# Operand loads in fewer pieces and moved against the steps, and a GpSimd cast in place of the values' casting loads

## The chip, the cores and the metric

The kernel runs on one core of a Trainium2 chip. The metric is the device time of one execution in microseconds. Before the change three executions took 695.05, 695.21 and 695.46 us, a median of 695.21. A further execution was profiled: it took 694.12 us, of which the trace spans 692.2 us from the first to the last instruction.

## The reference

```python
def _attn_ref(q, k, v, centroids):            # q, k, v: (2, 8, 768, 64), float32
    q_n = q / (norm(q) + 1e-6); k_n = ...; c_n = ...
    q_assign = argmax(einsum('bhsd,hcd->bhsc', q_n, c_n)); k_assign = ...   # 16 clusters a head
    mask = q_assign[:, :, :, None] == k_assign[:, :, None, :]
    scores = where(mask, scale * q @ k^T, -1e9)
    scores -= max(scores)
    attn = exp(scores); attn /= sum(attn) + 1e-9
    return attn @ v
def _moe_ref(x, U, V, w_ch1, w_ch2):          # mixing over tokens, then a feed-forward layer
    u = x + (x^T @ U @ V)^T
    return u + relu(u @ w_ch1) @ w_ch2
def _moe2_ref(x, w_in, conv_w, w_out):        # a gated layer with a convolution of width 3
    h = relu(x @ w_in)
    return (h * sigmoid(conv3(h))) @ w_out
```

The whole is `_moe2_ref(_moe_ref(attention))`. The change touches the attention alone.

## The kernel before, in words

The program has three stages: attention (from the start to about 300 us), the feed-forward layer, and the gated layer. In the attention two heads form a pair (index b for the batch, p for the pair, j = 0 or 1 for the head within it); there are 8 pairs, and each head has 6 query tiles of 128 rows. One query tile is one step n, so there are 96 steps, 12 to a pair; s is a step's number within its pair.

A product of float32 precision is made of two parts of the type fp32r, a rounded high half and the low half, which is the difference between the number and its rounded half. For scores the kernel keeps two tiles for each head. `cd` holds the rounded q and k on partitions 0 to 63 (and cluster rows on 64 to 79, which do the masking). `ab` holds 128 partitions: low q beside rounded k on one half of the partitions, rounded q beside low k on the other. One product with `ab` (L342) and one with `cd` (L353) give the scores of a step.

The rounded parts come by DMAs issued on the GpSimd queue, which cast while they move. `load_ops` (L108) loads the same 384 KB of one head three times: into both halves of `ab` and into `cd`. `load_raw` (L89) brings the unrounded rows of a pair (tiles rq, rk) by SyncE's queue. `split_ops` (L124) turns half of `ab` into low parts: two GpSimd subtractions for each head, raw minus rounded, in place. The values go the same way: `load_v` (L115) loads them unrounded into rv on SyncE's queue and rounded into vt with two casting DMAs on GpSimd's queue, and a GpSimd subtraction (L532, L633) puts the low half beside the rounded one.

A step (function `step`, L644) issues, in this order: the scores of step n + 2; a third of the value product of a group of three steps (`pv_mm`); on every third step the transposes that end a group (`fin_t`); the transposes of the exponentials (`t_mm`, L380); on ScalarE and VectorE their rounding and low half (`t_hi` L389, `t_lo` L393); the exponential of step n + 1 and the maximum of n + 2. At steps with (n - 4) divisible by 3, GpSimd adds 1e-9 to a group's three sums (L681), and `fin_x` (L423) ends the group before it: ScalarE copies the transposed result from PSUM into the tile `ats` (L426), VectorE takes the reciprocal of the sums (L429), GpSimd adds the two halves (L430) and multiplies by the reciprocal into X (L434, three times). The tile `ats` has one buffer, so ScalarE's next copy waits for GpSimd's last multiplication.

`prep` (L610) prepares the next pair beside the current one: loads of head 0 at s = 0, its split at s = 2, the values' loads at s = 3, loads of head 1 at s = 4 and its split at s = 5, cluster rows at s = 6, and the values' low half at s = 8. Before the loop, lines 526 to 532 do the same for the second head of pair 0 and its values. Every engine runs its instructions in the order in which they are written here; there is no scheduler. `a_ab` has 3 buffers, so at most three heads' operands live at once; rq, rk and vt have 2, rv has 1.

Of the kernel before, what the change touches and what calls it, by code (L numbers as in the profile page):

```python
# [15 lines left out]
F32 = mybir.dt.float32  # L16
# [8 lines left out]
P = 128  # L25
# [6 lines left out]
def tile_kernel(ctx: ExitStack, tc: tile.TileContext, qk, vv, cen, u_w, v_w, w1, w2, win, wout, conv, out):  # L32
    nc = tc.nc
    B, H, D, _, S = qk.shape
    NC = cen.shape[0] // H
    NP = H // 2
# [31 lines left out]
    a_e = att.enter_context(tc.tile_pool(name="a_e", bufs=3))  # L68
# [16 lines left out]
    raw = {}  # L85
    ops = {}
    vts = {}

    def load_raw(b, p, parts=1):  # L89
        rq, rk = raw[b, p] if (b, p) in raw else take_raw(b, p)  # L90
        h0 = 2 * p
        for i in range(parts):
            c = slice(i * S // parts, (i + 1) * S // parts)
            nc.sync.dma_start(out=rq[:, c], in_=qk[b, h0:h0 + 2, :, 0, c].rearrange("h d s -> (h d) s"))
            nc.sync.dma_start(out=rk[D:2 * D, c], in_=qk[b, h0, :, 1, c])
            nc.sync.dma_start(out=rk[0:D, c], in_=qk[b, h0 + 1, :, 1, c])

    def take_raw(b, p):
        raw[b, p] = tuple(a_raw.tile([P, S], F32, tag=t, name=t) for t in ("rq", "rk"))
        return raw[b, p]  # L100

    def take_ops(b, p, j):
        ab = a_ab.tile([P, 2, S], F32R, tag="ab", name="ab")
        cd = a_ab.tile([80, 2, S], F32R, tag="cd", name="cd")
        ops[b, 2 * p + j] = (ab, cd)
        return ab, cd

    def load_ops(b, p, j):  # L108
        h = 2 * p + j
        ab, cd = take_ops(b, p, j)  # L110
        nc.gpsimd.dma_start(out=ab[0:D], in_=qk[b, h])
        nc.gpsimd.dma_start(out=ab[D:2 * D], in_=qk[b, h])
        nc.gpsimd.dma_start(out=cd[0:D], in_=qk[b, h])

    def load_v(b, p):  # L115
        rv = a_v.tile([P, 2, NT, D], F32, tag="rv", name="rv", bufs=1)
        vt = a_v.tile([P, 2, NT, 2 * D], F32R, tag="vt", name="vt")
        nc.sync.dma_start(out=rv, in_=vv[b, p])
        for j in range(2):
            nc.gpsimd.dma_start(out=vt[:, j, :, 0:D], in_=vv[b, p, :, j])  # L120
        vts[b, p] = vt
        return rv, vt

    def split_ops(b, p, j, eng):  # L124
        rq, rk = raw[b, p]
        ab, _ = ops[b, 2 * p + j]
        q0, k0 = (0, D) if j == 0 else (D, 0)
        for r, i, p0 in ((rq, 0, q0), (rk, 1, k0)):
            eng.tensor_sub(ab[p0:p0 + D, i], r[p0:p0 + D], ab[p0:p0 + D, i])


    cent = acon.tile([P, 1, D], F32, name="cent")
# [60 lines left out]
    def split_first(half, which):  # L193
        c = slice(half * HS, (half + 1) * HS)
        if which == "k":
            nc.scalar.copy(cd0[0:D, 1, c], rk0[D:2 * D, c])
            nc.scalar.copy(ab0[0:D, 1, c], rk0[D:2 * D, c])
            nc.gpsimd.tensor_copy(ab0[D:2 * D, 1, c], rk0[D:2 * D, c])
            nc.vector.tensor_sub(ab0[D:2 * D, 1, c], rk0[D:2 * D, c], ab0[D:2 * D, 1, c])
        else:  # L200
            nc.scalar.copy(cd0[0:D, 0, c], rq0[0:D, c])
            nc.scalar.copy(ab0[D:2 * D, 0, c], rq0[0:D, c])
            nc.gpsimd.tensor_sub(ab0[0:D, 0, c], rq0[0:D, c], cd0[0:D, 0, c])
# [7 lines left out]
    def sims(b, p, tiles=range(NT)):  # L211
        rq, rk = raw[b, p]
        if (b, p) not in ohst:
            ohst[b, p] = {"pm": ps_t.tile([P, NT * 4, NC], F32, tag="t", name="sim")}
        pm = ohst[b, p]["pm"]
        for t in tiles:
            for i, (r, cb) in enumerate(((rq, cbq), (rk, cbk))):
                nc.tensor.matmul(
                    pm[:, 4 * t + 2 * i:4 * t + 2 * i + 2, :].rearrange("p g c -> p (g c)"),
                    r[:, t * P:(t + 1) * P], cb[:, p], start=True, stop=True,  # L220
                )

    def sims_onehot(b, p, part):

        v = ohst[b, p]
        if part == 0:
            v["mx"] = a_oh.tile([P, NT * 4, 1], F32, tag="mx", name="mx")
            v["eq"] = a_oh.tile([P, NT * 4, NC], BF16, tag="eq", name="eq")
            v["m2"] = a_oh.tile([P, NT * 4, 1], BF16, tag="m2", name="m2")
            v["oh"] = a_oh.tile([P, NT * 4, NC], BF16, tag="oh", name="oh")  # L230
        onehot_part(v, v["pm"], slice(0, NT * 4), part)
# [15 lines left out]
    def onehot_t(b, p):  # L247
        oh = ohst[b, p]["oh"]
        pt = ps_t.tile([4 * NC, S], BF16, tag="t", name="oht")
        for t in range(NT):  # L250
            nc.tensor.transpose(pt[:, t * P:(t + 1) * P], oh[:, 4 * t:4 * t + 4].rearrange("p g c -> p (g c)"), identb)
        ohst[b, p]["pt"] = pt

    def onehot_rows(b, p):
        pt = ohst.pop((b, p))["pt"]
        os_ = a_oh.tile([4 * NC, S], F32R, tag="os", name="os")
        nc.scalar.activation(os_, pt, AF.Identity, scale=ohs[:, 0:1], bias=ohs[:, 1:2])
        put_rows(b, p, os_, range(2))

    def put_rows(b, p, os_, heads):  # L260
        for j in heads:
            cd = ops[b, 2 * p + j][1]
            for i in range(2):
                r0 = (2 * i + j) * NC
                nc.sync.dma_start(out=cd[D:D + NC, i].bitcast(F32), in_=os_[r0:r0 + NC].bitcast(F32))
# [62 lines left out]
    st = {}  # L328
    X = {}

    def head_of(n):
        b, r = divmod(n, H * NT)
        h, t = divmod(r, NT)
        return b, h, t
# [87 lines left out]

    def fin_x(g):  # L423
        b, h, t0 = head_of(3 * g)
        at = a_e.tile([P, 3, 2, D], F32, tag="ats", name="ats", bufs=1)
        nc.scalar.copy(at, st.pop(("at", g)))  # L426
        sm = st.pop(("sum", g))
        rs = a_s.tile([P, 3, 1], F32, tag="rs", name="rs")
        nc.vector.reciprocal(rs[:, :, 0], sm)  # L429
        nc.gpsimd.tensor_add(at[:, :, 0], at[:, :, 0], at[:, :, 1])  # L430
        if h == 0 and t0 == 0:
            X[b] = xp.tile([P, NT, DM], F32, tag="x", name="x")
        for i in range(3):
            nc.gpsimd.tensor_tensor(  # L434
                out=X[b][:, t0 + i, h * D:(h + 1) * D], in0=at[:, i, 0],
                in1=rs[:, i].to_broadcast([P, D]), op=ALU.mult,
            )
# [48 lines left out]
    def pump(plan):  # L486

        for j in list(fly):
            j["at"] += 1
            if j["at"] in j["plan"]:  # L490
                j["plan"][j["at"]](j)
            if j["at"] == max(j["plan"]):
                fly.remove(j)
        if plan is THIN:
            free = not fly
        else:
            free = not fly or (fly[-1]["at"] > 1 and fly[-1]["plan"] is FLOW)
        if jobs and free:
            j = jobs.pop(0)
            j["at"], j["plan"] = 0, plan  # L500
            job_dma(j)
            fly.append(j)
# [21 lines left out]


    load_ops(0, 0, 1)
    rv0 = load_v(0, 0)
    first_pair()
    split_first(1, "q")
    sims(0, 1, range(2))  # L530
    split_ops(0, 0, 1, nc.gpsimd)
    nc.gpsimd.tensor_sub(rv0[1][:, :, :, D:2 * D], rv0[0], rv0[1][:, :, :, 0:D])  # L532


    u3 = mixc.tile([P, NT, 3, R], F32, name="u3")
# [74 lines left out]
    def prep(n):  # L610

        pair, s = divmod(n, 2 * NT)
        nxt = pair + 1
        if nxt < B * NP:
            b, p = divmod(nxt, NP)
            for part, at in enumerate((2, 2, 3, 4, 5) if nxt > 1 else (0, 0, 1, 2, 3)):
                if s == at and (nxt > 1 or part > 1):
                    sims_onehot(b, p, part)
            if s == 0:
                if nxt > 1:  # L620
                    load_raw(b, p)
                load_ops(b, p, 0)
            elif s == 2:
                split_ops(b, p, 0, nc.gpsimd)
            elif s == 3:
                st["rv"] = load_v(b, p)
            elif s == 4:
                load_ops(b, p, 1)
            elif s == 5:
                split_ops(b, p, 1, nc.gpsimd)  # L630
            elif s == 8:
                rv, vt = st.pop("rv")
                nc.gpsimd.tensor_sub(vt[:, :, :, D:2 * D], rv, vt[:, :, :, 0:D])  # L633
            if s == (6 if nxt > 1 else 5):
                onehot_t(b, p)
                onehot_rows(b, p)
        if n == NQ - 7:
            queue_chunk(1, lambda: wpc)
        if n >= NQ - 7:
            pump(FLOW)  # L640
        elif n % 2 == 0 and n > 0:
            pump(THIN)

    def step(n):  # L644
# [43 lines left out]
        if 0 <= n < NQ:  # L688
            prep(n)
# [190 lines left out]
    for i in range(len(order) + 2):  # L880
# [7 lines left out]
        if 0 <= i - 2:  # L888
            b, f = order[i - 2]
# [57 lines left out]
```

## Time and profile before

| | us |
|---|---|
| median of three executions | 695.21 (695.05 to 695.46) |
| profiled execution, device time | 694.12 |
| its span | 692.2 |
| TensorE busy | 666.3 (96%) |
| VectorE busy | 445.8 (64%) |
| ScalarE busy | 373.0 (54%) |
| GpSimd busy | 298.9 (43%) |

Times in rows are counted from the first instruction. In a timeline row the columns are start, duration, engine, line, operation, out<-in, shapes and count, and in brackets how long the engine sat idle before it and what ended that. PE is TensorE, PEld its weight loads, DVE VectorE, ACT ScalarE, POOL GpSimd and SP SyncE. A timeline row with a count above one runs from its first instruction to its last, other engines' rows being listed between them.

### The profile page before, as it was taken

How to read it: one execution, taken by the hardware profiler on the slowest of the kernel's cores; microseconds unless marked ns; L12 is line 12 of the kernel's file. 1: busy time of each engine (PE TensorE's matmuls, PEld its weight loads, DVE VectorE, ACT ScalarE, POOL GpSimd, SP SyncE). 2: the span in 40 equal slices, each digit the busy share in tenths (PEclk: the TensorE clock that was granted, in tenths of full speed). 3: DMA queues.
4: the chain of work that ended last, by engine and by line, in shares of the span. 5: the costliest groups of instructions: out<-in, count | busy, mean ns of one | idle time of the engine just before them, and what ended most of it. 6: DMA issues, size and time to landing. Idle time of an engine off the chain costs nothing.

```text
span 692.2 us, 10474 instructions
## 1 busy us (share of the span) xinstructions
PE 666.3 (96%) x3782; PEld 586.0 (85%) x3782; DVE 445.8 (64%) x833; ACT 373.0 (54%) x750; POOL 298.9 (43%) x392
## 2 busy tenths in 40 slices
PE   8949999999999999999999999999999999999997
PEld 6849999999898998888888888888887788888886
DVE  6837888797978798749831778775237645643400
ACT  6837888787777898424311333433133457653611
POOL 6647666676666642515621333332015634332300
PEclk9988999999999999999999999999999999999999
DMA  9895768685666610301210333442003000000111
GB/s 195 151 136 115 165 116 197 108 192 103 167 119 153 131 35 5 118 31 63 92 62 1 121 123 121 142 133 92 1 30 125 28 0 1 1 32 16 43 49 46
DMA packets 32131, 61.58 MB, mean 89 GB/s; under 512 B 15856, under 2 KB 19568, under 8 KB 32080
## 3 DMA queue, kind: packets, MB, share of 16 engines
q1 hardware_dynamic: 15936, 40.08, 19.6%
q0 software_dynamic: 16144, 20.84, 17.6%
q8 instruction: 30, 0.49, 0.3%
q14 instruction: 21, 0.17, 0.1%
HBM read 56.29 MB, written 3.15 MB: 86 GB/s over the span
## 4 chain that ended last, share of the span: by engine, by line
PE 78%; DVE 8%; issue 3%; DMA 3%; ACT 3%; POOL 2%; ACTq 0%; POOLq 0%; DVEq 0%
PE g L836 10%; PE tr L380 7%; PE pv L404 7%; PE h L713 5%; PE h L715 5%; PE h L714 5%; PE a L730 5%; PE a L729 5%; PE a L731 5%; PE sc L342 3%; PE sc L353 3%; PE po L870 3%; PE po L871 3%; PE po L872 3%; DMA ab<-in_qk_dram 3%
## 5 line engine op out<-in xcount | busy, mean ns | idle before, releaser
L518 POOL TENSOR_TENSOR wl<-wx,wh 128x512 fp32r<-128x512 f32 x48 | 63.0, 1314 | 114.8 <-ACT wh L517 114.5
L393 DVE TENSOR_TENSOR pl<-tr,ph 128x384 fp32r<-128x384 f32 x192 | 97.6, 549 | 21.5 <-ACT ph L389 20.3
L380 PE MATMUL tr<-identf,e 128*128 128x128 f32 x576 | 83.7, 278 | 16.5 <-ACT ats L426 11.4
L389 ACT CAST ph<-tr 128x384 fp32r<-128x384 f32 x192 | 83.5, 485 | 21.3 <-PE tr L380 20.5
L359 DVE TENSOR_SCALAR_CACHE_REDUCE e<-sc 128x768 f32<-128x768 f32 x96 | 90.8, 947 | 0.6 <-PE sc L353 0.6
L718 ACT ACTIVATE rh<-h 128x512 fp32r<-128x512 f32 (+1 forms) x52 | 29.3, 563 | 111.7 <-PE h L715 111.7
L371 ACT ACTIVATE e<-sc,nb 128x768 f32<-128x768 f32 x96 | 88.4, 921 | 1.0 <-DVE e L359 0.9
L380 PEld LDWEIGHTS tr<-identf,e 128*128 128x128 f32 x576 | 66.9, 142 | 25.9 <-ACT ats L426 12.6
L719 DVE SCALAR_TENSOR_TENSOR rl<-h,rh 128x512 fp32r<-128x512 f32 (+1 forms) x52 | 33.7, 648 | 82.9 <-ACT rh L718 82.8
L713 PE MATMUL h<-uh,wh 128*128 128x512 f32 (+1 forms) x208 | 78.1, 376 | 1.6 <-DVE rl L719 1.6
L729 PE MATMUL a<-rh,wh 128*128 128x512 f32 (+1 forms) x208 | 78.1, 376 | 0.5 <-DVE xa L745 0.5
L730 PE MATMUL a<-rl,wh 128*128 128x512 f32 (+1 forms) x208 | 77.8, 374 | 0.5 <-DVE rl L719 0.3
L731 PE MATMUL a<-rh,wl 128*128 128x512 f32 (+1 forms) x208 | 77.6, 373 | 0.0
L715 PE MATMUL h<-uh,wl 128*128 128x512 f32 (+1 forms) x208 | 77.6, 373 | 0.0
L714 PE MATMUL h<-ul,wh 128*128 128x512 f32 (+1 forms) x208 | 77.6, 373 | 0.0
L404 PE MATMUL pv<-ph,vt 128*128 128x384 f32 x192 | 66.0, 344 | 0.2 <-ACT asb L413 0.2
L404 PE MATMUL pv<-pl,vt 128*128 128x384 f32 x192 | 65.3, 340 | 0.0
L517 ACT CAST wh<-wx 128x512 fp32r<-128x512 f32 x48 | 29.8, 620 | 58.3 <-DVE wx L471 58.1
L342 PE MATMUL sc<-ab 128*128 128x384 f32 x192 | 57.4, 381 | 0.7 <-ACT e L371 0.4
L853 POOL TENSOR_TENSOR h<-h,cv 128x768 f32<-128x768 f32 x16 | 29.6, 1850 | 64.5 <-ACT cv L852 64.5
L467 DVE SCALAR_TENSOR_TENSOR wx<-wb,wx 128x512 int32<-128x512 int32 (+3 forms) x52 | 48.3, 928 | 11.4 <-ACT wb L458 9.4
L353 PE MATMUL sc<-cd 80*128 80x384 f32 x192 | 49.7, 341 | 0.0
(136 smaller groups left out, 1493.4 us busy)
## 6 DMA issues: line engine op xcount, KB each, us to landing
raw<-in_w_dram SPq DMA_DIRECT2D x32, 512.0 KB, 3.7
ab<-in_qk_dram POOLq DMA_DIRECT2D x30, 384.0 KB, 5.2
cd<-in_qk_dram POOLq DMA_DIRECT2D x15, 384.0 KB, 6.8
raw<-in_win_dram SPq DMA_DIRECT2D x8, 512.0 KB, 3.7
raw<-in_wout_dram SPq DMA_DIRECT2D x8, 512.0 KB, 3.7
rv<-in_vv_dram SPq DMA_DIRECT2D x8, 384.0 KB, 3.4
vt<-in_vv_dram POOLq DMA_DIRECT2D x16, 192.0 KB, 3.6
out_dram<-o SPq DMA_DIRECT2D x24, 128.0 KB, 1.8
```

The source lines that it names most:

```text
L359: nc.vector.tensor_scalar(out=e, in0=ps[:, :, 0:HS], scalar1=-SCALE, scalar2=3e38, op0=ALU.mult, op1=ALU.min, accum_out=nb,)
L371: nc.scalar.activation(e, ps[:, :, 0:HS], AF.Exp, scale=SCALE, bias=nb, accum_out=st["sum", n // 3][:, n % 3:n % 3 + 1])
L380: nc.tensor.transpose(pt[:, k, :], e[:, i, k * P:(k + 1) * P], identf)
L389: nc.scalar.copy(st["pt", n // 3][0][:, i * NK:(i + 1) * NK, n % 3, :], st["t", n, i])
L393: nc.vector.tensor_sub(lo, st.pop(("t", n, i)), hi)
L404: nc.tensor.matmul(acc, vt[:, h % 2, k, :], m[:, k].rearrange("p a b -> p (a b)"), start=(k == 0 and i == 0), stop=(k == NT - 1 and i == 1),)
L713: nc.tensor.matmul(ph, wh[:, k, ws], uh[g][:, k, ts], start=(k == 0), stop=False)
L714: nc.tensor.matmul(ph, wh[:, k, ws], ul[g][:, k, ts], start=False, stop=False)
L715: nc.tensor.matmul(ph, wl[:, k, ws], uh[g][:, k, ts], start=False, stop=(k == ND - 1))
L729: nc.tensor.matmul(accs[d][:, 0:n], wh[:, i, ds_], rh, start=(f == 0), stop=False)
L730: nc.tensor.matmul(accs[d][:, 0:n], wh[:, i, ds_], rl, start=False, stop=False)
L731: nc.tensor.matmul(accs[d][:, 0:n], wl[:, i, ds_], rh, start=False, stop=(f == NH - 1))
```

## The change

`load_ops` loads two and a half pieces for each head in place of three: the whole into `cd`, the whole into the upper half of `ab`, and into the lower half of `ab` only that one of q and k which stays rounded there. The low part on the lower half is now the raw rows minus `cd`, written into `ab`; the other subtraction is as before. `load_v` keeps only SyncE's load. A new function `split_v` makes the rounded half by a GpSimd copy with a cast (L122 of the changed kernel) and then the low half (L123). The first head of pair 1 is loaded before the loop; a later pair's first head, and its raw rows, are loaded at s = 10 of the pair two before it. The split of head 0 moves from s = 2 to s = 1, the loads of head 1 from s = 4 to 3, their split from s = 5 to 7, the values' load from 3 to 4. The tile `ats` gets a second buffer.

```diff
--- before.py
+++ after.py
@@ -108,25 +108,27 @@
     def load_ops(b, p, j):
         h = 2 * p + j
         ab, cd = take_ops(b, p, j)
-        nc.gpsimd.dma_start(out=ab[0:D], in_=qk[b, h])
+        nc.gpsimd.dma_start(out=cd[0:D], in_=qk[b, h])
         nc.gpsimd.dma_start(out=ab[D:2 * D], in_=qk[b, h])
-        nc.gpsimd.dma_start(out=cd[0:D], in_=qk[b, h])
+        nc.gpsimd.dma_start(out=ab[0:D, 1 - j], in_=qk[b, h, :, 1 - j])
 
     def load_v(b, p):
         rv = a_v.tile([P, 2, NT, D], F32, tag="rv", name="rv", bufs=1)
+        nc.sync.dma_start(out=rv, in_=vv[b, p])
+        return rv
+
+    def split_v(b, p, rv):
         vt = a_v.tile([P, 2, NT, 2 * D], F32R, tag="vt", name="vt")
-        nc.sync.dma_start(out=rv, in_=vv[b, p])
-        for j in range(2):
-            nc.gpsimd.dma_start(out=vt[:, j, :, 0:D], in_=vv[b, p, :, j])
+        nc.gpsimd.tensor_copy(vt[:, :, :, 0:D], rv)
+        nc.gpsimd.tensor_sub(vt[:, :, :, D:2 * D], rv, vt[:, :, :, 0:D])
         vts[b, p] = vt
-        return rv, vt
 
     def split_ops(b, p, j, eng):
-        rq, rk = raw[b, p]
-        ab, _ = ops[b, 2 * p + j]
-        q0, k0 = (0, D) if j == 0 else (D, 0)
-        for r, i, p0 in ((rq, 0, q0), (rk, 1, k0)):
-            eng.tensor_sub(ab[p0:p0 + D, i], r[p0:p0 + D], ab[p0:p0 + D, i])
+
+        ab, cd = ops[b, 2 * p + j]
+        lo, hi = raw[b, p][j], raw[b, p][1 - j]
+        eng.tensor_sub(ab[0:D, j], lo[0:D], cd[0:D, j])
+        eng.tensor_sub(ab[D:2 * D, 1 - j], hi[D:2 * D], ab[D:2 * D, 1 - j])
 
 
     cent = acon.tile([P, 1, D], F32, name="cent")
@@ -422,7 +424,7 @@
 
     def fin_x(g):
         b, h, t0 = head_of(3 * g)
-        at = a_e.tile([P, 3, 2, D], F32, tag="ats", name="ats", bufs=1)
+        at = a_e.tile([P, 3, 2, D], F32, tag="ats", name="ats", bufs=2)
         nc.scalar.copy(at, st.pop(("at", g)))
         sm = st.pop(("sum", g))
         rs = a_s.tile([P, 3, 1], F32, tag="rs", name="rs")
@@ -527,9 +529,10 @@
     rv0 = load_v(0, 0)
     first_pair()
     split_first(1, "q")
+    load_ops(0, 1, 0)
     sims(0, 1, range(2))
     split_ops(0, 0, 1, nc.gpsimd)
-    nc.gpsimd.tensor_sub(rv0[1][:, :, :, D:2 * D], rv0[0], rv0[1][:, :, :, 0:D])
+    split_v(0, 0, rv0)
 
 
     u3 = mixc.tile([P, NT, 3, R], F32, name="u3")
@@ -616,24 +619,22 @@
             for part, at in enumerate((2, 2, 3, 4, 5) if nxt > 1 else (0, 0, 1, 2, 3)):
                 if s == at and (nxt > 1 or part > 1):
                     sims_onehot(b, p, part)
-            if s == 0:
-                if nxt > 1:
-                    load_raw(b, p)
-                load_ops(b, p, 0)
-            elif s == 2:
+            if s == 1:
                 split_ops(b, p, 0, nc.gpsimd)
             elif s == 3:
+                load_ops(b, p, 1)
+            elif s == 4:
                 st["rv"] = load_v(b, p)
-            elif s == 4:
-                load_ops(b, p, 1)
-            elif s == 5:
+            elif s == 7:
                 split_ops(b, p, 1, nc.gpsimd)
             elif s == 8:
-                rv, vt = st.pop("rv")
-                nc.gpsimd.tensor_sub(vt[:, :, :, D:2 * D], rv, vt[:, :, :, 0:D])
+                split_v(b, p, st.pop("rv"))
             if s == (6 if nxt > 1 else 5):
                 onehot_t(b, p)
                 onehot_rows(b, p)
+        if s == 10 and pair + 2 < B * NP:
+            load_raw(*divmod(pair + 2, NP))
+            load_ops(*divmod(pair + 2, NP), 0)
         if n == NQ - 7:
             queue_chunk(1, lambda: wpc)
         if n >= NQ - 7:
```

GpSimd's queue at the start of the loop, before the change, from the last piece of head 0's split (L203): ab_209 is the second head of pair 0, ab_338 and ab_450 are the two heads of pair 1, vt_215 and vt_417 the values of pairs 0 and 1.

```order
L203 TENSOR_TENSOR ab_196<-rq_111,cd_197 64x384
L129 TENSOR_TENSOR ab_209<-rq_111,ab_209 64x768
L129 TENSOR_TENSOR ab_209<-rk_112,ab_209 64x768
L532 TENSOR_TENSOR vt_215<-rv_214,vt_215 128x12x64
L111 DMA ab_338<-in_qk_dram 64x1536
L112 DMA ab_338<-in_qk_dram 64x1536
L113 DMA cd_339<-in_qk_dram 64x1536
L129 TENSOR_TENSOR ab_338<-rq_180,ab_338 64x768
L129 TENSOR_TENSOR ab_338<-rk_181,ab_338 64x768
L120 DMA vt_417<-in_vv_dram 128x6x64 x2
L681 TENSOR_SCALAR sum_302<-sum_302 128x3
```

The same place on GpSimd in the changed kernel: ab_209 and vt_291 are pair 0's, ab_279 with cd_280 and ab_415 with cd_416 the two heads of pair 1.

```order
L205 TENSOR_TENSOR ab_196<-rq_111,cd_197 64x384
L111 DMA cd_280<-in_qk_dram 64x1536
L112 DMA ab_279<-in_qk_dram 64x1536
L113 DMA ab_279<-in_qk_dram 64x768
L130 TENSOR_TENSOR ab_209<-rk_112,cd_210 64x768
L131 TENSOR_TENSOR ab_209<-rq_111,ab_209 64x768
L122 CAST vt_291<-rv_214 128x12x64
L123 TENSOR_TENSOR vt_291<-rv_214,vt_291 128x12x64
L130 TENSOR_TENSOR ab_279<-rq_180,cd_280 64x768
L131 TENSOR_TENSOR ab_279<-rk_181,ab_279 64x768
L111 DMA cd_416<-in_qk_dram 64x1536
L112 DMA ab_415<-in_qk_dram 64x1536
```

The three load issues of pair 1's first head have moved ahead of pair 0's splits, a cast stands ahead of the values' low half, and the splits of pair 1's first head follow four instructions behind its loads, not directly.

A few rows further on GpSimd, before the change: the loads of pair 1's second head (ab_450, cd_451), its split, and the first group's end (sum, ats, x).

```order
L111 DMA ab_450<-in_qk_dram 64x1536
L112 DMA ab_450<-in_qk_dram 64x1536
L113 DMA cd_451<-in_qk_dram 64x1536
L129 TENSOR_TENSOR ab_450<-rq_180,ab_450 64x768
L129 TENSOR_TENSOR ab_450<-rk_181,ab_450 64x768
L681 TENSOR_SCALAR sum_384<-sum_384 128x3
L430 TENSOR_TENSOR ats_558<-ats_558 128x3x64
L434 TENSOR_TENSOR x_563<-ats_558,rs_560 128x64 x3
L633 TENSOR_TENSOR vt_417<-rv_416,vt_417 128x12x64
```

The same place in the changed kernel, from the last of those loads (ab_415, the second head of pair 1):

```order
L113 DMA ab_415<-in_qk_dram 64x768
L682 TENSOR_SCALAR sum_306<-sum_306 128x3
L682 TENSOR_SCALAR sum_385<-sum_385 128x3
L432 TENSOR_TENSOR ats_552<-ats_552 128x3x64
L436 TENSOR_TENSOR x_557<-ats_552,rs_554 128x64 x3
L130 TENSOR_TENSOR ab_415<-rk_181,cd_416 64x768
L131 TENSOR_TENSOR ab_415<-rq_180,ab_415 64x768
L122 CAST vt_589<-rv_449 128x12x64
L123 TENSOR_TENSOR vt_589<-rv_449,vt_589 128x12x64
L682 TENSOR_SCALAR sum_472<-sum_472 128x3
```

The first group's sums and its end (ats, x) now stand between the loads and the split that waits for them; before, they stood behind that split.

## Rows read from the trace of the kernel before

**Rows 1.** The page's chain that ended last, its shares of the span by engine:
```profile
PE 78%; DVE 8%; issue 3%; DMA 3%; ACT 3%; POOL 2%; ACTq 0%; POOLq 0%; DVEq 0%
```

**Rows 2.** Busy time by stretch: bounds, length, each engine (count), clock, DMA share, GB/s:
```profile
41.00:52.00 11.00, 1.61 (x8) 0.96 (x6) 1.31 (x3) 1.36 (x4) 6.59 (x8) 0.71 0.48 82
52.00:60.00 8.00, 7.93 (x42) 7.54 (x42) 6.27 (x16) 6.29 (x15) 4.75 (x13) 0.75 0.78 187
60.00:100.00 40.00, 39.46 (x289) 38.38 (x288) 33.03 (x77) 31.32 (x74) 28.88 (x45) 1.00 0.61 119
```

**Rows 3.** Timeline of all engines, 28 to 58 us, the first group's copy and the longest gap:
```profile
33.28 0.49 ACT L426 COPY ats<-at 128x384 f32<-128x384 f32 x1
...
49.10 0.18 DVE L429 RECIPROCAL rs<-sum 128x3 f32<-128x3 f32 x1 [8.90 <-POOL sum L681]
50.64 0.48 ACT L426 COPY ats<-at 128x384 f32<-128x384 f32 x1 [11.10 <-POOL x L434]
```

**Rows 4.** Timeline of GpSimd, 14 to 56 us:
```profile
14.73 0.99 POOL L203 TENSOR_TENSOR ab<-rq,cd 64x384 fp32r<-64x384 f32 x1 [3.87 <-ACT cd L201]
...
19.98 2.00 POOL L532 TENSOR_TENSOR vt<-rv,vt 128x768 fp32r<-128x768 f32 x1 [0.21 <-POOL ab L129]
21.93 0.57 POOL L111 DMA_DIRECT2D ab<-in_qk_dram  x1
...
28.57 1.83 POOL L129 TENSOR_TENSOR ab<-rq,ab 64x768 fp32r<-64x768 f32 x1 [5.01 <-DVE e L359]
...
34.34 0.57 POOL L111 DMA_DIRECT2D ab<-in_qk_dram  x1
...
45.09 1.80 POOL L129 TENSOR_TENSOR ab<-rq,ab 64x768 fp32r<-64x768 f32 x1 [9.11 <-DMA ab<-in_qk_dram]
```

**Rows 5.** Timeline of TensorE, 39 to 59 us, step transposes of n = 10 to 13:
```profile
39.55 0.82 PE L380 MATMUL tr<-identf,e 128*128 128x128 f32 x6
51.18 1.88 PE L380 MATMUL tr<-identf,e 128*128 128x128 f32 x6 [9.39 <-ACT ats L426]
55.56 1.02 PE L380 MATMUL tr<-identf,e 128*128 128x128 f32 x6
58.14 0.82 PE L380 MATMUL tr<-identf,e 128*128 128x128 f32 x6
```

**Rows 6.** The same, 82 to 91 us, steps 22 and 25:
```profile
83.20 0.82 PE L380 MATMUL tr<-identf,e 128*128 128x128 f32 x6
...
89.72 0.82 PE L380 MATMUL tr<-identf,e 128*128 128x128 f32 x6
```

**Rows 7.** GpSimd's groups: shapes xcount | busy, mean ns | idle before, releaser:
```profile
L120 POOL DMA_DIRECT2D vt<-in_vv_dram x16 | 14.0, 880 | 1.5 <-PE pv L404 1.5
L633 POOL TENSOR_TENSOR vt<-rv,vt 128x768 fp32r<-128x768 f32 x7 | 12.9, 1842 | 0.0
L198 POOL CAST ab<-rk 64x384 fp32r<-64x384 f32 x2 | 1.0, 504 | 0.1
L541 POOL COPY u<-wx 128x192 f32<-128x192 f32 x3 | 0.9, 343 | 0.1
```

**Rows 8.** Timeline of TensorE's weight loads, first value product of pair 0:
```profile
24.00 0.19 PEld L404 LDWEIGHTS pv<-ph,vt 128*128 128x128 f32 x1
```

**Rows 9.** The tile ab: its DMAs from issue to landing:
```profile
DMA to landing us min/median/max: 3.9/5.2/10.0
```

**Rows 10.** Timeline of GpSimd, 84 to 87 us, around s = 10 of pair 1:
```profile
84.93 0.80 POOL L434 TENSOR_TENSOR x<-ats,rs 128x64 f32<-128x64 f32 x3
85.67 0.58 POOL L111 DMA_DIRECT2D ab<-in_qk_dram  x1
```

**Rows 11.** Timeline of VectorE, one instruction with two SBUF inputs, GpSimd idle, then busy:
```profile
512.89 0.69 DVE L467 SCALAR_TENSOR_TENSOR wx<-wb,wx 128x512 int32<-128x512 int32 x1
518.48 1.77 DVE L467 SCALAR_TENSOR_TENSOR wx<-wb,wx 128x512 int32<-128x512 int32 x1 [1.19 <-ACT wb L458]
```

**Rows 12.** Timeline of GpSimd, what it ran beside the second of these:
```profile
515.71 5.69 POOL L751 TENSOR_TENSOR ul<-xa,uh 128x512 fp32r<-128x512 f32 x4 [36.31 <-ACT uh L750]
```

## The prediction

> **What bounds the kernel now.** The page's chain comes first: 78% of the span is TensorE's own work, and the next largest share is 8% [rows 1]. No step of this change shortens a product, so only waits of TensorE can be won. The table of stretches, read next, shows where they lie. From 60 to 100 us TensorE is busy 39.46 of 40 us; from 41 to 52 us it is busy 1.61 of 11, and there and in the 8 us behind it the granted clock averages 0.71 and 0.75, where it is 1.00 afterwards [rows 2]. One hole, then, at the end of pair 0, with a slow stretch behind it.
>
> The timelines of this stretch say whose hole it is. TensorE's transposes of step 11 wait 9.39 us for ScalarE's copy into `ats` [rows 5]; that copy waits 11.10 us for GpSimd's multiplication of the group before, which reads the one `ats` buffer, and VectorE's reciprocal waits 8.90 us for GpSimd's sum [rows 3]. GpSimd itself had stood 9.11 us before the split of head 3 (the second head of pair 1), whose loads it had begun to issue at 34.34 us; 5.01 us more had gone before the split of head 2, for loads begun at 21.93 [rows 4]. The split stands right behind its loads on an in-order engine, and the sums and group ends stand behind the split. So what decides is GpSimd's lag in the first pair, and two other engines hang on it by two separate ties.
>
> What the hole costs: from step 10 to step 13 the transposes advance 58.14 - 39.55 = 18.59 us [rows 5]; the same four places one pair later take 89.72 - 83.20 = 6.52 us [rows 6]. The difference, **12.07 us**, holds the 9.39 us of waiting, and nearly all the rest is step 11, which takes 55.56 - 51.18 = 4.38 us at the lower of the two clock levels (1.2 of 2.4 GHz).
>
> **The change part by part.**
>
> *Head 2's loads, ahead of pair 0's splits.* GpSimd ends L203 at 14.73 + 0.99 = 15.72 us [rows 4]. It then issues two whole pieces at 0.57 us and a half piece, which lies between nothing and 0.57 [rows 4] and which I take at half: 17.2 us. The two splits of head 1 took it from there to the values' subtraction in 19.98 - 15.72 = 4.26 us, 0.3 of it waiting for a load [rows 4], so they end near 21.1. The cast of the values (128x768) does not occur before. The nearest rows are a cast of 384 elements, 0.504 us, and copies of 192, 0.343 [rows 7]; carried on by their difference this gives 0.83, by twice the cast 1.0, and I take 0.95; as an upper end it costs as much as the subtraction of the same shape, 1.84 us [rows 7], as a lower end 0.504. Then the subtraction, 2.00 us [rows 4]: the values are ready at about 24.2 to 24.4 us, with the upper end 25.3, where TensorE loads its first value weights at 24.00 [rows 8] and the values were ready at 21.98. **This cover is gone: +0.3 us**, between 0 and 1.3.
>
> *Splits of head 2.* Its loads, begun at 15.72, have 8.5 us before GpSimd comes to them at 24.4; the tile's loads take 5.2 us in the median, 10.0 at most [rows 9]. The earlier wait of 5.01 us goes. The splits end near 28.1.
>
> *Head 3's loads and its split, now parted.* The loads are issued from 28.1 to 29.7, six microseconds before their old place. Then come the sums, and the first group's end, for which ScalarE's copy is there at 33.28 + 0.49 = 33.8 [rows 3]; an addition and 0.80 us of multiplications [rows 10] keep GpSimd until about 35.2, and only then it turns to the split, two times 1.83 us [rows 4]. By the median the first piece is there at 33.3, by the maximum at 38.1, so the split waits 0 to 3 us. It ends between 38.9 and 42, the values between 41.8 and 45, the next sum a quarter of a microsecond later. VectorE asks for that sum at step 13, which without the hole is near 39.55 + 6.52 = 46 us. So even the slowest load in this trace leaves 0.8 us, and **the hole goes: -12.07 us**. Since TensorE then has no rest there, the cause of the low clock is gone too. Once it goes, the next late thing would be what binds TensorE in every pair; the reference stretch of 6.52 us already contains that.
>
> *The second buffer of `ats`.* By itself it would cut ScalarE's tie to the multiplication, but not VectorE's to the sum: the reciprocal starts at 49.10 and the copy at 50.64 [rows 3], so it is worth about 1.5 us alone. Together with the new order it adds nothing to the sum; it is slack.
>
> *The steady pairs.* The loads at s = 10 change little there: GpSimd had nothing between the multiplication of s = 10 and the loads of s = 0, and issued the loads at 85.67, directly behind the multiplication begun at 84.93 [rows 10]. Sixteen issues of casting loads at 0.880 us go and seven casts come (the eighth is pair 0's), and 15 third pieces shrink [rows 7]; GpSimd is not what TensorE waits for in these pairs, where it is busy 28.88 of 40 us [rows 2]. Zero.
>
> *A shared port.* VectorE's L467, which reads two tiles in SBUF, takes 0.69 us with GpSimd idle and 1.77 beside a GpSimd instruction with two inputs [rows 11, 12]. Such instructions of VectorE run in the attention too, and the new casts and moved splits can meet other ones than before. A cast hides nothing by this row and the moved splits may come out better or worse; bounds are -2 and, if each of seven casts held VectorE for its 0.95 us on the path, +6.7. I take +0.2, near zero, because the GpSimd time removed (14.0 us of issues) is larger than that added, and VectorE had 7 of 40 us to spare [rows 2].
>
> The Trainium skill has a rule here that speaks against the change: "SBUF — State Buffer", section "Who interferes with whom", says that a VectorE instruction with two SBUF inputs contends with a GpSimd instruction that reads SBUF, and that whoever issues first keeps the other out. The trace agrees in kind: 0.69 against 1.77 us. By the rule descriptor writing, which reads no operand, would not have held up such VectorE instructions and a cast would; then the trade is not neutral, and the sum would be 682.4 + 6.7 = 689 at worst instead of 682.6, both in the profiled execution's terms.
>
> **Sum.** Of the profiled execution: 694.12 - 12.07 + 0.3 + 0.2 = 682.55 us. That execution lies 1.09 us below the median of 695.21, which gives **683.6 us** in the terms of the median, 1.7% less.
>
> **Rivals.**
>
> *The hole shrinks but stays.* If the first piece of head 3 lands later than 11 us after its issue (past 39.1 us), the sum behind split and values passes 46 us and VectorE waits. For: at 28 to 36 us cluster rows and pair 2's raw rows move too, as they did at 34 us, when the longest load took 10.0 us [rows 9]. Against: the values' casting loads, two pieces just ahead of it then, are gone. A landing after 15 us, half as late again as the longest seen, leaves 4 us of waiting, with some slow clock 687.6 to 689.
>
> *The port.* The casts and splits meet VectorE's work in the later pairs, which is fuller: up to 6.7 us by the bound above, so 684.5 to 690.
>
> *It does not do what it says.* Had the hole another root than GpSimd's lag, only `ats` would count: 1.5 us, 693.7. The two ties named above both end in GpSimd; I see little for it.
>
> *Slower: GpSimd falls behind in every pair.* At s = 1 the split waits for loads issued three steps, about 6.5 us, before; behind it stand head 1's loads, and the sum and group end of s = 4, for which VectorE asks at s = 7. Loads that take 10.0 us would hold GpSimd 3.5 us; with the split's 3.7 and 1.4 for the next loads' issues that is 8.6 us against the 6.5 of three steps [rows 6], so 2.1 us in each of six pairs, 13 us: 696.6. It decides from loads of 8 us on. Against it: the median landing of 5.2 us [rows 9], and fewer bytes in flight now.
>
> **How the numbers follow.** The forecast (the hole goes whole) 0.82, with its own range of 682.3 to 685.2, from 0 to 1.3 us for the values' lateness and about a microsecond of port luck either way. The hole in part 0.06; the port 0.06; not what it says, or no change, 0.03; slower 0.03. The range, 682.0 to 687.0, takes in the forecast's bounds and half of the next two cases. A measurement of this kernel tells about 0.2%, 1.4 us, from no change: faster 0.94, within it 0.03, slower 0.03.
>
> **What would show it right or wrong.** Right: TensorE busy over 10 of 11 us from 41 to 52 us, granted clock 1.00 to the end of the attention, no wait of ScalarE's `ats` copy or VectorE's reciprocal for GpSimd over 1 us, GpSimd's waits of 5.01 and 9.11 us for loads gone, the cast near 0.95 us and the first value weights loaded at 24.2 to 24.5 us. Wrong: a gap over 2 us at steps 10 to 16, VectorE's two-input instructions longer in pairs 3 to 6, or the later stages no longer the same length.

## The result and the profile after

The changed kernel takes 686.68 us, the median of 7 runs (685.75 to 692.4), beside 695.21 for 7 runs of the kernel before. The ratio is 0.9898, with a 95% interval of 0.9873 to 0.9923: 7.1 us gained (5.4 to 8.8) where 11.6 were forecast. The medians lie further apart, by 8.5 us; the ratio is near that of the means (687.6 and 694.7), of which the execution of 692.4 us raises the first. The median lies inside the range on record and outside the likeliest case's own (682.3 to 685.2); 695.21 less 7.1, which is 688.1, lies 1.1 us above the range. The profiled execution took 687.84 us, 5.3 more than the sum of 682.55.

The hole is gone. Stretches of the changed kernel, in the columns of [rows 2]:

```profile
28.00:41.00 13.00, 12.63 (x85) 11.48 (x84) 11.18 (x25) 11.28 (x27) 7.47 (x13) 1.00 0.82 177
41.00:52.00 11.00, 10.86 (x79) 10.45 (x77) 10.31 (x24) 8.91 (x21) 8.44 (x16) 1.00 0.55 125
52.00:60.00 8.00, 8.00 (x61) 7.90 (x61) 6.68 (x16) 6.01 (x14) 6.46 (x14) 1.00 0.49 98
60.00:100.00 40.00, 37.99 (x269) 35.92 (x268) 33.41 (x74) 32.56 (x75) 21.43 (x35) 1.00 0.46 101
```

TensorE is busy 10.86 of 11 us where it was busy 1.61, at full clock. The last row holds the surprise: from 60 to 100 us it is busy 37.99 us where [rows 2] has 39.46, although GpSimd has 7.5 us less to do there.

GpSimd in the first pair, answering to [rows 4] (timeline of the changed kernel):

```profile
15.91 0.55 POOL L111 DMA_DIRECT2D cd<-in_qk_dram  x1
...
21.30 1.04 POOL L122 CAST vt<-rv 128x768 fp32r<-128x768 f32 x1
22.42 1.83 POOL L123 TENSOR_TENSOR vt<-rv,vt 128x768 fp32r<-128x768 f32 x1
24.21 1.83 POOL L130 TENSOR_TENSOR ab<-rq,cd 64x768 fp32r<-64x768 f32 x1
26.12 2.03 POOL L131 TENSOR_TENSOR ab<-rk,ab 64x768 fp32r<-64x768 f32 x1
28.09 0.55 POOL L111 DMA_DIRECT2D cd<-in_qk_dram  x1
...
35.44 0.60 POOL L432 TENSOR_TENSOR ats<-ats 128x192 f32<-128x192 f32 x1 [5.16 <-ACT ats L428]
36.12 0.79 POOL L436 TENSOR_TENSOR x<-ats,rs 128x64 f32<-128x64 f32 x3
36.87 1.83 POOL L130 TENSOR_TENSOR ab<-rk,cd 64x768 fp32r<-64x768 f32 x1
...
43.51 0.23 POOL L682 TENSOR_SCALAR sum<-sum 128x3 f32<-128x3 f32 x1
```

Neither split has an idle time in front of it: the waits of 5.01 and 9.11 us for loads are gone. The direction has turned, too: GpSimd now waits for ScalarE's copy (5.16 us at 35.44), where ScalarE waited 11.10 for GpSimd [rows 3].

Where the missing time went is read from the transposes of steps 0, 12 and 84, which begin pair 0, pair 1 and pair 7. TensorE's timeline of the changed kernel, with steps 10 and 13 (41.47 and 48.42) and the three gaps between:

```profile
17.93 1.48 PE L382 MATMUL tr<-identf,e 128*128 128x128 f32 x6
...
41.47 0.82 PE L382 MATMUL tr<-identf,e 128*128 128x128 f32 x6
...
45.97 0.82 PE L382 MATMUL tr<-identf,e 128*128 128x128 f32 x6
48.42 0.82 PE L382 MATMUL tr<-identf,e 128*128 128x128 f32 x6
...
72.52 0.55 PE L382 MATMUL tr<-identf,e 128*128 128x128 f32 x3 [0.93 <-DVE pl L395]
...
105.35 0.55 PE L382 MATMUL tr<-identf,e 128*128 128x128 f32 x3 [0.93 <-DVE pl L395]
...
170.33 1.01 PE L382 MATMUL tr<-identf,e 128*128 128x128 f32 x6 [1.09 <-DVE pl L395]
...
245.32 0.82 PE L382 MATMUL tr<-identf,e 128*128 128x128 f32 x6
```

The kernel before, steps 0 and 84 (step 12 stands in [rows 5] at 55.56):

```profile
17.05 0.82 PE L380 MATMUL tr<-identf,e 128*128 128x128 f32 x6
...
251.56 0.82 PE L380 MATMUL tr<-identf,e 128*128 128x128 f32 x6
```

| us | until step 0 | pair 0 | pairs 1 to 6 | rest of the span |
|---|---|---|---|---|
| before | 17.05 | 38.51 | 196.00 | 440.6 |
| after, by the sum on record | 17.05 | 26.94 | 196.00 | 440.6 |
| after | 17.93 | 28.04 | 199.35 | 440.6 |

Of 5.3 us, 3.35 lie in pairs 1 to 6, 1.1 in pair 0 and 0.9 ahead of it. All three gaps end with VectorE's low half (`pl`), and ahead of each stands the same instruction. VectorE and GpSimd of the changed kernel at the first gap and, below, in pair 3, where there is none:

```profile
69.83 1.83 POOL L131 TENSOR_TENSOR ab<-rq,ab 64x768 fp32r<-64x768 f32 x1
69.83 2.04 DVE L465 TENSOR_SCALAR wx<-raw 96x384 int32<-96x384 int32 x1
71.90 1.02 DVE L395 TENSOR_TENSOR pl<-tr,ph 128x384 fp32r<-128x384 f32 x2
...
135.61 0.43 DVE L465 TENSOR_SCALAR wx<-raw 128x512 int32<-128x512 int32 x1
135.62 2.13 POOL L131 TENSOR_TENSOR ab<-rq,ab 64x768 fp32r<-64x768 f32 x1
```

L465 (`job_low`) shifts the words of a later stage's weights, once in each pair at s = 8; it has one input in SBUF. The second subtraction of head 1's split, which the change moved from s = 5 to 7, now begins within 0.01 us of it. Where GpSimd is first, VectorE's instruction takes nearly as long as both together (2.04 us, against 1.83 + 0.36); where VectorE is first, GpSimd's takes 0.3 us more. In pairs 1, 2 and 4 GpSimd is first (2.04, 2.03, 2.11 us), in pairs 3, 5 and 6 VectorE. In the kernel before, in pair 1, the same instruction (L463 there) came 0.17 us behind the end of the split (GpSimd's and VectorE's timelines):

```profile
77.58 1.81 POOL L129 TENSOR_TENSOR ab<-rk,ab 64x768 fp32r<-64x768 f32 x1
...
79.56 0.36 DVE L463 TENSOR_SCALAR wx<-raw 96x384 int32<-96x384 int32 x1
```

The Trainium skill, "SBUF — State Buffer", section "Who interferes with whom", goes on, behind the rule on two inputs, to say that a `tensor_scalar` too can, where its operands allow it, run in a mode that takes the port shared with GpSimd, that the order of issue decides, and that the loser is shut out whole. The trace agrees in effect: 2.04 us against 0.36; no view of it shows the mode or the port.

### The profile page after: what moved, and what is told of

It is laid out like the page before. It is cut to its first block, busy times and chain, and to the rows that moved or that the text cites. A ratio compares the mean times of both kernels' runs of the same rounds, so it can differ in the third digit from the quotient of the medians.

```text
span 685.9 us, 10453 instructions
## 1 busy us (share of the span) xinstructions
PE 666.7 (97%) x3782; PEld 586.1 (85%) x3782; DVE 451.3 (66%) x833; ACT 373.1 (54%) x750; POOL 292.0 (43%) x384
## 4 chain that ended last, share of the span: by engine, by line
PE 78%; DVE 9%; issue 4%; ACT 4%; POOL 3%; DMA 0%; ACTq 0%; POOLq 0%; DVEq 0%
PE g L837 10%; PE tr L382 8%; PE pv L406 7%; PE h L714 5%; PE h L716 5%; PE h L715 5%; PE a L731 5%; PE a L730 5%; PE a L732 5%; PE sc L344 3%; PE sc L355 3%; PE po L871 3%; PE po L872 3%; PE po L873 3%; PE sim L220 2%
## 5 line engine op out<-in xcount | busy, mean ns | idle before, releaser
L395 DVE TENSOR_TENSOR pl<-tr,ph 128x384 fp32r<-128x384 f32 x192 | 97.6, 549 | 17.7 <-ACT ph L391 16.9
L432 POOL TENSOR_TENSOR ats<-ats 128x192 f32<-128x192 f32 x32 | 19.6, 611 | 90.4 <-ACT ats L428 85.2
L469 DVE SCALAR_TENSOR_TENSOR wx<-wb,wx 128x512 int32<-128x512 int32 (+3 forms) x52 | 49.0, 942 | 11.4 <-ACT wb L460 9.5
```

What stands on the lines that cost most here:

```text
L395: nc.vector.tensor_sub(lo, st.pop(("t", n, i)), hi)
```

## The experiments

The theory after the result: the hole went as forecast, and a race between L465 and the moved subtraction, decided within 0.01 us, gives part of it back in some pairs: whichever of the two begins first holds the other up. Rivals: the second `ats` buffer did the work, or hurts; the smaller volume of loads did it; the pairs are slower because the split comes later, whatever VectorE does.

**e1, the second `ats` buffer alone, in the kernel before.**

```diff
-        at = a_e.tile([P, 3, 2, D], F32, tag="ats", name="ats", bufs=1)
+        at = a_e.tile([P, 3, 2, D], F32, tag="ats", name="ats", bufs=2)
```

> The kernel before with one edit: the tile ats has two buffers. If GpSimd's lag is the root of the gap at step 11 and reaches TensorE by two ties (ScalarE's copy into ats, VectorE's reciprocal behind GpSimd's sum), the second tie keeps it: gap of 7 to 8 us in place of 9.4, 693.7 us, 1.5 us faster. If the one buffer is the root, the gap goes and the time is 683 to 687 us.

Measured: 694.27 us (692.76 to 696.02), ratio 1.0001 (0.9986 to 1.0017). Timelines of GpSimd, VectorE and TensorE:

```profile
44.34 1.80 POOL L129 TENSOR_TENSOR ab<-rq,ab 64x768 fp32r<-64x768 f32 x1 [8.00 <-DMA ab<-in_qk_dram]
...
48.36 0.17 DVE L429 RECIPROCAL rs<-sum 128x3 f32<-128x3 f32 x1 [5.20 <-POOL sum L681]
...
49.73 0.90 PE L380 MATMUL tr<-identf,e 128*128 128x128 f32 x3 [4.65 <-DVE pl L393]
```

The copy no longer waits, but the second tie does: the reciprocal waits 5.20 us for GpSimd's sum, which stands behind the split and its loads (8.00). A gap of 4.65 us stays where 9.39 were, less than the 7 to 8 expected. Pair 0 is 2.6 us shorter in this profile (35.92 against 38.51) and pairs 1 to 6 are 1.2 longer; over the runs the 1.5 us expected do not show. Of two ties the buffer cuts one.

**e2, the changed kernel with one `ats` buffer.** The same line turned back:

```diff
-        at = a_e.tile([P, 3, 2, D], F32, tag="ats", name="ats", bufs=2)
+        at = a_e.tile([P, 3, 2, D], F32, tag="ats", name="ats", bufs=1)
```

> The changed kernel with the second buffer of ats taken away again. If the new order alone removes GpSimd's lag, the buffer is slack: 686.7 us within 1 us, no gap over 2 us in the first pair, ScalarE's copies wait for GpSimd under 1 us each. If the buffer carries a part of the gain, a gap comes back at steps 10 to 16 and the time is 688 us or more.

Measured: 686.48 us (683.51 to 688.32), ratio 0.9881 (0.9855 to 0.9907), as the changed kernel; the copy waits nowhere for GpSimd. With the new order the buffer is slack. The profiled execution, the fastest (683.51), happened to win the race in all six pairs: pairs 1 to 6 took 195.01 us.

**e3, the new order with the old volume: three whole pieces, and the values' high half by casting loads.** The lines that make the tile vt in `load_v` and hand it on are left out here.

```diff
-        nc.gpsimd.dma_start(out=ab[0:D, 1 - j], in_=qk[b, h, :, 1 - j])
+        nc.gpsimd.dma_start(out=ab[0:D], in_=qk[b, h])
 # load_v
+        for j in range(2):
+            nc.gpsimd.dma_start(out=vt[:, j, :, 0:D], in_=vv[b, p, :, j])
 # split_v
-        nc.gpsimd.tensor_copy(vt[:, :, :, 0:D], rv)
```

> The changed kernel's order, with three whole pieces for each head again and the values' high half by two casting loads again (issued at s = 4), no cast on GpSimd. Theory order: the gain comes from where loads and splits stand, not from what is loaded: no gap over 2 us at steps 10 to 16, and the time is the changed kernel's 686.7 us within 1.5 us (the race at s = 8 stands as it did). Rival volume: with 21 MB on the casting queue again in place of 15 the first pair's loads land late and a part of the gap comes back: 689 us or more.

Measured: 686.83 us (684.78 to 690.57), ratio 0.9908 (0.9879 to 0.9936). Its stretch at the hole's place:

```profile
41.00:52.00 11.00, 11.00 (x83) 10.89 (x82) 8.72 (x22) 8.15 (x19) 7.19 (x11) 1.00 0.71 106
```

No hole: the order removes it, not the volume. VectorE's reciprocal still waits 1.19 us once for GpSimd's sum, which it does nowhere in the changed kernel, so the smaller volume seems to add margin. Pairs 1 to 6 take 199.41 us here too, with other instructions hit (L249, the one-hot product, takes 1.25 us in the mean where the changed kernel's L247 takes 0.55).

**e4, head 1's split back at s = 5.**

```diff
             elif s == 3:
                 load_ops(b, p, 1)
-            elif s == 4:
                 st["rv"] = load_v(b, p)
-            elif s == 7:
+            elif s == 5:
                 split_ops(b, p, 1, nc.gpsimd)
-            elif s == 8:
+            elif s == 6:
                 split_v(b, p, st.pop("rv"))
```

> The changed kernel with head 1's split moved from s = 7 back to s = 5 and the values' cast and low half from s = 8 to 6 (their load from 4 to 3), into the 6.3 us in which GpSimd stands idle before s = 7. Theory port: the missing gain is VectorE's L465 (first step of a weight word, at s = 8), which takes 2.0 us in place of 0.4 when the second subtraction of the split starts just ahead of it, in pairs 1, 2 and 4; then L465 is 0.36 to 0.43 us in every pair, the gaps of 0.9 to 1.1 us at steps 9 and 8 go, and the time is 682.5 to 683.5 us, 3 to 4 us below the changed kernel. Rival start: the missing gain went into the start (half clock from 16.2 to 19.6 us, values late) and the late gaps are chance; then 686.7 us as before.

Measured: 688.1 us (687.08 to 690.03), ratio 0.9909 (0.9886 to 0.9932): missed. Groups of VectorE from 45 to 245 us (shapes xcount | busy, mean ns):

```profile
L247 DVE TENSOR_TENSOR oh<-eq,m 128x384 bf16<-128x384 bf16 x6 | 9.3, 1547 | 0.0
L465 DVE TENSOR_SCALAR wx<-raw 128x512 int32<-128x512 int32 x4 | 1.7, 428 | 0.1
L465 DVE TENSOR_SCALAR wx<-raw 96x384 int32<-96x384 int32 x2 | 0.7, 356 | 0.1
```

L465 is short in every pair, as expected; but the split now stands beside another instruction, the one-hot product L247 with two SBUF inputs, which takes 1.55 us in place of 0.55, six times. The collision was moved, not removed: pairs 1 to 6 take 200.06 us.

**e5, L465 moved instead, from s = 8 to 10.**

```diff
-    THIN = {0: job_dma, 2: job_base, 3: job_low, 4: job_high, 5: job_sign, 6: job_put}
+    def job_two(j):
+        job_low(j)
+        job_high(j)
+    THIN = {0: job_dma, 2: job_base, 4: job_two, 5: job_sign, 6: job_put}
```

> The changed kernel with GpSimd's order untouched; VectorE's L465 is moved instead, from s = 8 to s = 10, directly ahead of the next step of the same word. Theory port: the collision at s = 8 is gone from VectorE's side, the gaps of 0.9 to 1.1 us in pairs 1, 2 and 4 go; at s = 10 it may meet GpSimd's addition (0.6 us) for less; 683 to 685 us. Rival, that the split at s = 7 delays TensorE by something else than L465 (loads, sums, operands late): 686.7 us.

Measured: 685.58 us (685.37 to 687.25), ratio 0.9875 (0.9855 to 0.9895). The late gaps are gone and pairs 1 to 6 take 196.65 us, 2.7 less than in the changed kernel. In pair 0 L465 now meets the values' low half (L123, 1.85 us from 43.10 on):

```profile
43.31 1.75 DVE L465 TENSOR_SCALAR wx<-raw 128x192 int32<-128x192 int32 x1
```

**e6, e4 with the one-hot product one step earlier.**

```diff
-            for part, at in enumerate((2, 2, 3, 4, 5) if nxt > 1 else (0, 0, 1, 2, 3)):
+            for part, at in enumerate((2, 2, 3, 4, 4) if nxt > 1 else (0, 0, 1, 2, 3)):
```

> The kernel of e4 (split at s = 5, values at 6) with VectorE's last cluster instruction L247 moved from s = 5 to s = 4. In e4 L465 was short in every pair, and instead L247, which reads two tiles in SBUF, took 1.5 to 1.6 us in place of 0.55 beside the moved split, in pairs 1 to 6. Theory port: at s = 4 it is ahead of the split, both collisions are gone: 682 to 684 us, faster than both kernels. Rival (a split at s = 5 costs by itself, by waiting for its loads): 687 to 688 us as e4.

Measured: 684.58 us (684.32 to 687.31), ratio 0.9877 (0.9854 to 0.99), a little above what was expected. The group of e4's collision, same stretch:

```profile
L247 DVE TENSOR_TENSOR oh<-eq,m 128x384 bf16<-128x384 bf16 x6 | 3.6, 600 | 0.2
```

Pairs 1 to 6 are down to 196.4 us from e4's 200.06, so that was e4's loss.

**e7, 0.1 us of idle GpSimd work ahead of the second subtraction.** A memset of one column that nothing reads; all else as in the changed kernel, but for the line that makes the tile `pause`, left out here and in e8. It decides the race for VectorE.

```diff
         eng.tensor_sub(ab[0:D, j], lo[0:D], cd[0:D, j])
+        if j == 1 and p + b > 0:
+            nc.gpsimd.memset(pause[:, 0:1], 0.0)
         eng.tensor_sub(ab[D:2 * D, 1 - j], hi[D:2 * D], ab[D:2 * D, 1 - j])
```

> The changed kernel with a memset of one column (about 0.1 us) on GpSimd between the two subtractions of head 1's split. Theory race for the shared port: in the changed kernel L465 on VectorE and the second subtraction on GpSimd start within 10 ns of each other, and whoever is first holds the other out; with GpSimd 0.1 us later VectorE is always first: L465 takes 0.4 us in pairs 1 to 7 and 683 to 685 us, 2 to 3 us below the changed kernel, by an added instruction. Rival (the late gaps are another wait, of loads or operands): 686.7 us or a little more.

**e8, the mirror: 0.06 us of idle VectorE work ahead of L465.** It decides the race for GpSimd.

```diff
+        if j["plan"] is THIN:
+            nc.vector.memset(pause[:, 1:2], 0.0)
         nc.vector.tensor_scalar(out=x, in0=j["raw"][:, :, 0], scalar1=29, scalar2=None, op0=ALU.logical_shift_right)
```

> The changed kernel with a memset of one column (about 0.06 us) on VectorE ahead of L465 in the attention. Theory race: GpSimd's second subtraction is now always first, L465 takes 1.8 to 2.1 us in each of pairs 1 to 6, a gap of about 1 us follows in each: 688 to 691 us, 2 to 4 us above the changed kernel. Rival (another wait, or chance): 686.7 us and a few tenths.

Measured: e7 **683.0 us** (682.72 to 683.09), ratio 0.9844 (0.982 to 0.9869), faster than both kernels; e8 691.71 us (691.5 to 693.46), ratio 0.9976 (0.996 to 0.9991). In e7, GpSimd and VectorE at pair 1 (their L133 and L468 are L131 and L465), the groups from 45 to 245 us, and TensorE's transposes of steps 12 and 84:

```profile
69.60 0.09 POOL L132 MEMSET pause<- 128x1 f32 x1
69.77 2.02 POOL L133 TENSOR_TENSOR ab<-rq,ab 64x768 fp32r<-64x768 f32 x1
...
69.73 0.36 DVE L468 TENSOR_SCALAR wx<-raw 96x384 int32<-96x384 int32 x1
```
```profile
L468 DVE TENSOR_SCALAR wx<-raw 128x512 int32<-128x512 int32 x4 | 1.7, 428 | 0.1
L468 DVE TENSOR_SCALAR wx<-raw 96x384 int32<-96x384 int32 x2 | 0.7, 356 | 0.1
```
```profile
45.91 0.82 PE L385 MATMUL tr<-identf,e 128*128 128x128 f32 x6
...
240.60 0.82 PE L385 MATMUL tr<-identf,e 128*128 128x128 f32 x6
```

In e8 the same place, groups and transposes:

```profile
71.36 1.83 POOL L131 TENSOR_TENSOR ab<-rq,ab 64x768 fp32r<-64x768 f32 x1
...
71.39 0.06 DVE L467 MEMSET pause<- 128x1 f32 x1
71.48 1.92 DVE L468 TENSOR_SCALAR wx<-raw 96x384 int32<-96x384 int32 x1
```
```profile
L468 DVE TENSOR_SCALAR wx<-raw 128x512 int32<-128x512 int32 x4 | 8.0, 1988 | 0.1
L468 DVE TENSOR_SCALAR wx<-raw 96x384 int32<-96x384 int32 x2 | 3.8, 1920 | 0.1
```
```profile
47.54 0.82 PE L383 MATMUL tr<-identf,e 128*128 128x128 f32 x6
...
251.20 0.82 PE L383 MATMUL tr<-identf,e 128*128 128x128 f32 x6
```

VectorE wins all six pairs in e7 and loses all six in e8. Pairs 1 to 6 take 194.69 and 203.66 us: 9.0 us for six lost races, 1.5 each, and the medians differ by 8.7. The runs of the changed kernel, 685.75 to 692.4, begin above all of e7's and end within those of e8 (691.5 to 693.46), and its scatter of 6.7 us in 7 runs shrinks to 0.4 in the 5 of e7. That the pairs are slower for the late split as such is refuted: e7 has the split at the same step.

**e9 and e10, the kernel before and the changed kernel, unedited, one profiled execution more of each.** They ask whether the hole is the kernel's or one execution's, and whether the count of lost races gives the time.

> The kernel before, profiled a second time. If the gap at step 11 is the kernel's and not that execution's, it is there again: 8 to 11 us between steps 10 and 12 beyond the later pairs' pace, 691 to 697 us. If the first profile was an odd one, the gap is under 5 us.

> The changed kernel, profiled a second time. Theory race: which engine is first at s = 8 differs from the first profile in at least one of pairs 1 to 6, by nothing that the program says; each pair lost costs about 1.5 us, so the time is 683.0 plus 1.5 for each, 683 to 692 us. Rival (fixed waits): the same three pairs lose again and the time is 687.8 within 0.5 us.

Measured: 695.33 and 686.66 us. TensorE in the kernel before, at step 11:

```profile
52.34 1.88 PE L380 MATMUL tr<-identf,e 128*128 128x128 f32 x6 [8.99 <-ACT ats L426]
```

The hole is there again (8.99 us; 9.39 in [rows 5]). In the changed kernel only pair 5 loses the race, by 0.01 us:

```profile
199.90 1.83 POOL L131 TENSOR_TENSOR ab<-rq,ab 64x768 fp32r<-64x768 f32 x1
...
199.91 2.10 DVE L465 TENSOR_SCALAR wx<-raw 128x512 int32<-128x512 int32 x1
```

One race lost would be 683.0 + 1.5 = 684.5 us, so the count of races alone misses by 2.2. The rest lies at the start: step 0 begins at 19.29 us against 17.25 in e7, 2.0 later, and 686.5 is within 0.2 of what was measured. That close a fit is partly luck: against e7, pair 5 is 1.83 us longer, not 1.5, and pair 0 is 0.6 shorter.

## Why the prediction was half right

*The hole: right, its mechanism whole.* TensorE is busy in it, the clock is 1.00, both waits of GpSimd for loads are gone and neither tie holds an engine up. From step 10 to step 13 the transposes advance 48.42 - 41.47 = 6.95 us where they took 18.59, so the hole's term measured 11.64 us of the 12.07 forecast. e1 shows that there were two ties, e3 that the order of loads and splits is the cause, e2 that `ats` is slack, e9 that the hole belongs to the kernel. Which of the moves it takes, the loads further ahead or the split further behind, was not run apart.

*The values' half: its times right, its cost not met.* The cast takes 0.863 us in the mean of eight (0.95 estimated, 1.04 for the first), and the values are ready at 24.25 us (24.2 to 24.4; the recorded terms themselves, 21.1 + 0.95 + 2.00, make 24.05). The first value weights are loaded at 25.37, not 24.2 to 24.5, since step 0 itself came late. So TensorE did not wait for the values, and the +0.3 us set down for it was not paid.

*The steady loads: right.* In pairs 1 to 6 no engine waits for a result of GpSimd's, and the rival "GpSimd falls behind in every pair" did not show.

***A shared port*: the step that failed.** It took +0.2 us, "near zero, because the GpSimd time removed (14.0 us of issues) is larger than that added, and VectorE had 7 of 40 us to spare". It measured 3.35 us in pairs 1 to 6 of the profiled execution, and e7 and e8 show it to be anything from -1.3 to +7.7 against the 196.00 us of the kernel before, past the bound of +6.7. Neither reason bears on it. What counts is not how long GpSimd is busy but which of VectorE's instructions begins inside one long GpSimd instruction; the change took away issues, beside which no such wait was seen (in the kernel before L245, with two SBUF inputs, begins inside a load's issue in each of pairs 1 to 6 and takes 0.55 us), and moved 1.83 us subtractions onto new neighbours. The new casts, which the bound was worked out from, lengthened no instruction of VectorE's. Nor do VectorE's spare microseconds help, since the held instruction stands right ahead of the low half for which TensorE's transposes wait. The rival of the port had the right price (684.5 to 690) and too small a chance, 0.06, and the sign of being wrong watched only instructions with two inputs. Of these L247 is unchanged in pairs 1 to 6 (0.554 us, before 0.551), and L469 changes little in sum (0.52 to 0.85 us in pairs 1 and 2, 0.89 to 0.80 in pairs 3 to 6); the one that was hit hardest has one input. e4 then showed the two-input kind as well.

*The start: not foreseen.* Step 0 begins 0.88 us late and lasts 20.09 - 17.93 = 2.16 us, against 18.41 - 17.05 = 1.36. TensorE from 16 to 20 us in the kernel before, in its repetition e9, and in the changed kernel:

```profile
16.00:20.00 4.00, 3.65 (x23) 3.28 (x24) 3.80 (x9) 3.50 (x10) 3.68 (x3) 1.00 2.44 177
```
```profile
16.00:20.00 4.00, 3.65 (x15) 3.44 (x15) 2.79 (x6) 2.44 (x7) 3.83 (x3) 0.58 1.87 149
```
```profile
16.00:20.00 4.00, 3.65 (x16) 3.44 (x16) 2.68 (x6) 2.34 (x7) 3.92 (x5) 0.57 0.72 174
```

The clock is at the lower of its two levels for 3.4 of these 4 us in the changed kernel and in e9, so the kernel before has this stretch in some executions too. The prediction took a rest of TensorE's for the cause of a low clock; here there was none directly ahead, for from 12 to 16 us TensorE was busy 4.00 of 4 us in both. Why the clock fell is open. Each of the nine profiles with the new order has one or two such stretches that begin between 8.9 and 17.7 us; of the three with the old order e9 has one, and e1 one that begins at 24.9. Whether the change makes it likelier is open. It is worth some 1.7 us (0.88 ahead of step 0 and 0.80 in it), and 0.7 us more of pair 0 are steps 9 and 11, where L465 ran 1.25 us beside the split of head 3 and L469 1.20 beside the values' low half.

e7 at 683.0 us comes within 0.6 of the forecast, partly by chance: it still pays for the slow start, and its pairs 1 to 6 are 1.3 us shorter than before's 196.00, in which L463 took 0.84 and 0.83 us in place of 0.43 beside the addition L430 in pairs 4 and 6; the rest of the 1.3 was not traced.

## What to carry to other kernels

When a long GpSimd instruction is moved, list VectorE's SBUF-to-SBUF instructions at the new place, one-input shifts among them, and price each overlap at up to the whole GpSimd instruction on the path; average spare time does not cover it. If two such instructions start within a few hundredths of a microsecond, an added instruction of 0.1 us on the engine that should lose can settle the order; here that gained more than moving the work onto the next neighbour (683.0 us against 684.6 to 688.1 in e4 to e6). A kernel whose runs scatter by 1% may hold a race of this kind: compare the same instruction's duration pair by pair. Scatter alone does not show one: the kernel before ranges over 0.8% in the runs beside e7, and in none of its profiles does a split's subtraction hold L463 up.

## What the runs showed of the hardware

- An int32 shift on VectorE with one SBUF input takes 0.36 to 0.43 us alone and 1.92 to 2.11 behind a GpSimd subtraction of 1.83 us that began up to 0.12 us earlier. The other way round GpSimd loses only 0.2 to 0.3 us (2.02 to 2.14).
- The hold-up depends on what GpSimd does: beside a load's issue of 0.55 us on GpSimd a VectorE instruction with two SBUF inputs took its usual 0.55 us, beside a split's subtraction 1.5 to 1.6 (e4).
- The order at 0.01 us distance differs from pair to pair and from execution to execution of one kernel.
- An extra 0.09 us instruction on GpSimd, once in each of pairs 0 to 6, made the kernel 3.7 us faster (by ratio to the kernel before 0.9844 against 0.9898, with intervals that just do not meet); one of 0.06 us on VectorE in the same pairs made it 5.0 slower.
